# Transposing the softmax matrix by DMA instead of by matmul in a two-layer recurrent attention kernel

## The chip, the cores and the metric

The kernel runs on one core of a Trainium2 chip. The metric is device time in microseconds, the median of several runs; lower is better. A profiled execution gives the trace that is read here; its times are measured from the start of its span.

## What is computed

One block is a segment-recurrent attention followed by a gated feed-forward network (FFN), and it is applied twice with the same weights. The sequence has 2048 rows of 576 numbers, 32 heads of 128, an FFN of 4608.

```python
for s in range(n_seg):                     # 64 segments of 32 rows
    h = concatenate([mem, x[s]])           # 8 memory rows + 32 rows
    q, k, v = h @ Wq, h @ Wk, h @ Wv       # 32 heads of 128
    p = softmax(where(mask, q @ k.T * scale, -1e9))
    o = einsum(p @ v, Wo)
    mem = o[:8]                            # carried to the next segment
    outs.append(o[8:])
x = x + A(layernorm(x)); x = x + B(layernorm(x))    # B: (silu(x@w1) * (x@w3)) @ w2
x = x + A(layernorm(x)); x = x + B(layernorm(x))
```

Each segment needs the memory rows of the one before, so the attention is a chain of 64 links in each layer.

## The kernel before

**Steps.** The second layer runs eight segments behind the first (LAG). A step t does segment t of layer 0 and segment t - 8 of layer 1 together, 72 steps in all; in 56 of them both layers are there ("both"), in 16 one ("single"). The 32 heads are done in four groups of eight (g = 0 to 3). The FFN of finished rows, and the V of coming ones, are spread between the attention's pieces. The weights of the attention stay on the chip; those of the FFN are loaded again and again on SP's queue.

**A group.** Q and K are computed transposed into two PSUM banks (letters Q, and q for the contraction's tail), copied to QKT, and multiplied to scores (S). On VectorE and ScalarE follow the mask's addition, the row maximum and its subtraction, the exponential (sm_exp, on ScalarE), the row sum and its reciprocal, and the product with the reciprocal (sm_pb), which is written to PB, the softmax matrix P in bf16. In PB a row is a query (rows 0 to 39 are one layer's, 64 to 103 the other's) and a column is one of 128 rows of V, which hold both layers' keys and values in places that alternate with the step's parity (role). sm_pb writes only the columns of each row's own keys, in two to four instructions; the others must be zero.

**P transposed.** PV needs P with its keys on the partitions. ptr (letter T) does eight matmuls, PB as the stationary operand and fold, two 40 x 40 identities one above the other, as the moving one: the two layers' rows are added into the same 40 columns of one bank, 320 columns for eight heads. pt_ev evicts the bank twice, once for each layer, into PTS, each time times a column of slots (1 where the V row belongs to that layer, 0 elsewhere), on ScalarE or VectorE. In single steps it copies two halves of 160 columns with no mask. PV (P) then multiplies V by both layers' 80 columns; its result goes to OT, and Wo follows (O, tail o).

**Buffers.** PB has two buffers and PTS one. After each group's transpose GpSimd sets that PB to zero again (pb_zero, 128 x 1024).

**The order.** The program is a list of nodes with an engine, a duration, dependencies and buffers (make_nodes). plan (line 75) sends them out in time by an estimate; for TensorE the order is fixed by a string of letters (FIRST, then FOUR eleven times, then LAST), and every engine executes its nodes in the order that plan gives them. The letters are: m, a, b, n, p transposes of activations; Q q queries and keys; S scores; T the transpose of P; P P times V; O o the output projection; X x V v G g the values; F f the FFN's first matmuls; W w its second, for the two layers. FOUR covers four steps. Nodes marked AD go to ScalarE or VectorE, whichever plan finds free; the numbers in a node are plan's own estimates. A matmul node may use the whole array or column or row tiles of it; plan counts 0.098 us for a change (SWITCH).

All elementwise instructions are recorded at the two helper lines 594 (ScalarE) and 597 (VectorE), all matmuls at line 591. SP's DMAs are at line 600, those of ScalarE's queue at 603, which at present are four loads at the start, and those of GpSimd at 606.

Of the kernel before, what the change touches and what calls it, by code (L numbers as in the profile page):

```python
# [13 lines left out]
P = 128  # L14
# [20 lines left out]
POOLS = {"bank": 8, "qkt": 4, "sme": 2, "pb": 2, "pts": 1, "ot": 4,  # L35
# [158 lines left out]
def ewh(*ns):  # L194
# [5 lines left out]
    "maQQQqqQqqSQqTqSqQQQqSSvVXxPTPTOPOTOoPooOoQqqqqQQSQqqvSVQQTQSqqPQOTSPoXTOPToxPOOooQqqqqQQSQQSvqVQTqqQSQqPSaOTPTO"  # L200
    "PTooPOOooQQqqqqQSQVvSqqQQQqqQTSSPXTOPTOPoToxPOOooQQpQqqVvqqSnQQSfFFqqfQQqSTQqfPFTWPSFTOOooPFTffPOOooWQqqqqQQFSQF"
    "SQffqVvqqQWTQSFxfqfQFSPXTWPFTfOPOTFPOOooooWQqfqQQSFQfqqVvSQqqfFWTQqfQSFPQqfTOSPFOTWPFTOPfoooOoFfqqQQQSWQqqvVSFfq"
    "qQQTWqqSQQPTSOoPbaOTXPxTOPooxOoXqqpQQQSVqqnQvfFSTQqqQQPSFfqqfQTFOPSWTFfPOOTFPWOooooffFQQQqqqWSGFfgqQQqfFSTQPQQqq"
    "qfFSWGTSfgGPFggTGOPOTFPOOooooWVvfqqQQQSFqqffFQQWTSFfqqQPQfqqSFQWTOfPSTaFoOPWOTFPffFOoooWQQqqqqQSbQgqqGSQQTQPQTgq"
    "qSGSOPGggTGPOTOPoooOoQqqppQQQSvqqVnnQQqqSFSffqTFQPQqWTFSPffOwTFPOTFPOWOwooooFffqqQQQSWwQFfgqqGSFqqfQQTWQPQSFffqq"
    "FGTgSwPGfggTGPFTOPOWOOowoooFqqfQQwWQaQfqqSFSvVfqqQFQTFqqfPQTQwSWFSfPOOTFPwTWffFPOOooooWwqqqQQQbSQqqgqGSQTQPQQqgq"
    "TSGSGPggGTOPOTOPoooOo"
# [5 lines left out]
LAST = (  # L213
    "QQpQqqqQSqQpnQqqVvTSSnQFffqqFPQTOwPoSWTffFPFTOPOOoooFqqqfQQwWQQfqfSFSFqGQQqqgTQQPWwFqgfTSSGGPFfggfFTGOPOTWPOOwoF"
    "oooFfqqfQQQwvSqqVQQWQqqSFTSqfqQPQWTOPSwFTFPffOTOwPWOooooFFqqffQQwQQqqvSWVSFqqfQQTWPQTqqSVQvPOSTbOPxwOoTooPOoXqQp"
    "QpqqvVQSQqqnQnSQQqqFTSfqfPQTOPSFTFPOWTOPwOooooFqffqQQQSQQqqqvVSTQQqqFSffqFPQWSwTFPffTOPFOTwPOOoWoooFqfqqQQQFSQfq"
    "xvXVwWSTFPQffqqQWQTSwFFPfqqQOSwWTFOPffTFPOWOwooooFQQvfqqVqqQSQWFSwFffqqQQQSTWQqPqTPSOTOPowOToboPxOoXqqqQQQpSvVqq"
    "qQQSnQTFfqQFSPfqQOSTFfPowTFPfOTOPFOfooowQQqqqfQQSqFSVvqqQwQFTSQffqqQPFTSXPwTOPOTFPOOooooFfxfVvqqQQQSQqqqfQSFQqqq"
    "QSTQwSPFTOffPFTOPwTOPfooOooFQqqqQQSqqqQQSQvVQTSfFQqqPwTFSPfTOFPOTOPoofOoopwFnfffFFwFwfffFFFwffFFwffFFwffFFwfFffF"
    "wFwfffFFFfww"  # L220
# [11 lines left out]
def make_nodes(em, nseg, pools, o=Opt, dma_bw=230e3, load_bw=400e3):  # L232
# [26 lines left out]
    ld_m0 = node("ACT", 0.1, em.load_m0(), prio=-90, name="m0", lat=2.5)  # L259
    ld_t = [load("ldt", kb(3 * R64, 4096), -10.0, em.load_tails(0)), node("ACT", 0.1, em.load_tails(1), prio=-120, name="ldt", lat=6.0)]  # L260
    node("ACT", 0.1, em.load_tails(2), prio=-80, name="ldt", lat=6.0)
# [48 lines left out]
    def v_nodes(name, t, k, prio, tail_at, emit, strips, deps, tail_deps, free):  # L310

        modes = ("col", "quad") if strips[0][3] == R64 else ("c32", "oct")
        b = banks()
        m_ = node("PE", 8 * 0.2158, emit(b, False), deps=deps, prio=prio, mode=modes[0], acq=b, name=name)
        n = node("PE", 0.2158, emit(b, True), deps=deps + tail_deps, prio=prio + tail_at, mode=modes[1], acq=b, name=name + "t")
        reads_ht.setdefault(t, []).extend([m_, n])
        for r in (0, 1):
            outs = em.v_parts(strips, r)
            b[r].users = len(outs)
            for p0, width, row, blk in outs:  # L320
                e = node("AD", (0.49, 0.6), em.v_ev(b[r], p0, width, row, blk), deps=[m_, n] + free.get(blk // 2, []), prio=prio + 0.01 * (blk // 2),
                         rel=[b[r]], name=name + "e")
                vx_ev.setdefault((name, t, blk // 2), []).append(e)
        return [m_, n]
# [16 lines left out]
    def vg_out(t, g, b, deps, row):  # L341

        return [node("AD", (0.49, 0.6), em.v_ev(b[r], row, R64, row, 2 * g + r), deps=deps, prio=t + o.vm + 0.01 * g + (0.05 if row == 0 else 0.0), rel=[b[r]],
                     name="VGe") for r in (0, 1)]

    def vx_pair(t, prio):
# [5 lines left out]
        for k in ((0, 1) if both(t) else (0,)):  # L352
            v_nodes("VX", t, k, prio + 0.01 * k, o.vxt, (lambda k: lambda b, tail: em.vx(t, k, b, tail))(k), em.vx_strips(t, k), deps, [], free)

    def step(t):
# [17 lines left out]
        for g in range(NG):  # L373
# [52 lines left out]
            me[f"SC{g}"], me[f"TR{g}"], me[f"PV{g}"], me[f"WO{g}"] = sc, tr, pv, wo  # L426
# [100 lines left out]
    def x_in(g):  # L527
        xn = Slot("xn")
        ld = node("DMA" if g else "ACT", 0.8 if g else 0.1, em.load_xn(g, xn), deps=reads_ht.get(4 * g - 3, [])[:1], prio=4 * g - 3.0 if g else -100, acq=[xn],
                  name="ldxn", lat=2.5)  # L530
# [31 lines left out]
SW = 2 * QW  # L562

# [4 lines left out]
class Emitter:  # L568
# [431 lines left out]
    def sm_pb(self, t, g, sme, pb):  # L1000
        def f(n):
            for kd, key, c0, w in self.p_at(t):
                rs = slice(64 * kd, 64 * kd + QW)
                X, rec = self.T.SME[rs, sme.i], self.T.STAT[rs, sme.i]
                self.v("tensor_tensor", self.T.PB[rs, pb.i, :, c0:c0 + w], X[:, :, key:key + w],
                       rec.unsqueeze(2).to_broadcast([QW, GH, w]), op=ALU.mult)
        return f

    def pb_zero(self, pb):
        return lambda n: self.ch("POOL", self.nc.gpsimd.memset(self.T.PB[:, pb.i], 0.0))  # L1010
# [4 lines left out]
    def ptr(self, t, g, pb, b):  # L1015

        def f(n):
            for j in range(GH):
                self.mm(self.bk(b)[:, j * QW:(j + 1) * QW], self.T.PB[0:104, pb.i, j, :], self.T.fold[0:104, :], True, True)
        return f  # L1020

    def pt_ev(self, t, g, m, b, pts):

        def f(n):
            src = self.bk(b)[:, 0:GH * QW]
            if not self.both(t):
                w = 4 * QW
                self.cp(n, self.T.PTS[:, pts.i, 0, m * w:(m + 1) * w], src[:, m * w:(m + 1) * w])
                return
            dst = self.T.PTS[:, pts.i, m, :]  # L1030
            keep = self.T.slots[:, role(t), m ^ role(t):(m ^ role(t)) + 1]
            if n.by == "ACT":
                self.act(dst, src, ACT.Copy, scale=keep)
            else:
                self.v("tensor_scalar", dst, src, keep, None, op0=ALU.mult)
        return f
# [75 lines left out]
    def yts(self, t, ls, tail):  # L1112
        def f(n):
            yT, _ = self.yT(t)
            for li in ls:
                j = (t - LAG * li) % 4
                c0 = self.ycol(t, self.kind(t, li), False)
                if not tail:
                    self.cp(n, self.T.YTS[:, li, 0:4, j * SEG:(j + 1) * SEG], yT[:, 0:4, c0:c0 + SEG])
                else:  # L1120
                    self.v("tensor_tensor", self.T.YTS[R64:P, li, 4, j * SEG:(j + 1) * SEG], yT[0:R64, 4, c0:c0 + SEG],
# [3 lines left out]
    def post_tr(self, li, g, b):  # L1125
        def f(n):

            for db in (4, 3, 2, 1, 0):
                d0 = min(db * P, D - P)
                self.mm(self.bk_bf(b, D)[:, d0:d0 + P], self.T.YTS[:, li, db, :], self.T.ident[:, 0:P], True, True, is_transpose=True)  # L1130
# [79 lines left out]
def kernel(  # L1210
# [41 lines left out]
    T.fold = sp.tile([P, QW], BF, name="fold")  # L1252

    T.slots = sp.tile([P, 2, 2], F32, name="slots")

# [16 lines left out]
    T.YO = sp.tile([R64, 2 * QW], F32, name="YO")  # L1272
    T.YTS = sp.tile([P, 2, 5, P], BF, name="YTS")
# [11 lines left out]
    nc.gpsimd.memset(T.fold[:], 0.0)  # L1285
    for r in (0, R64):
        nc.gpsimd.affine_select(out=T.fold[:], in_=T.fold[:], compare_op=ALU.not_equal, fill=1.0, base=-r,
                                pattern=[[-1, QW]], channel_multiplier=1)

    nc.gpsimd.memset(T.slots[:], 0.0)  # L1290
    for e, kd, lo, hi in ((0, 1, 24, 80), (1, 0, 72, 112)):
        inside, outside = T.slots[:, e, kd:kd + 1], T.slots[:, e, 1 - kd:2 - kd]
        nc.gpsimd.memset(inside, 1.0)
        nc.gpsimd.affine_select(out=inside, in_=inside, compare_op=ALU.is_ge, fill=0.0, base=-lo, pattern=[[0, 1]], channel_multiplier=1)
        nc.gpsimd.affine_select(out=inside, in_=inside, compare_op=ALU.is_ge, fill=0.0, base=hi - 1, pattern=[[0, 1]], channel_multiplier=-1)
        nc.gpsimd.tensor_scalar(outside, inside, -1.0, 1.0, op0=ALU.mult, op1=ALU.add)

# [54 lines left out]
```

## Time and profile before

| | before |
|---|---|
| runs, median (lowest to highest) | 2704.19 us (2703.2 to 2704.23) |
| profiled execution | 2708.0 us |
| its span | 2705.0 us |
| mean granted TensorE clock | 0.997 |
| HBM read | 308.49 MB, 115 GB/s over the span |
| share of the 16 DMA engines taken by SP's queue | 38.5% |
| stretch 0 to 250 us: PE busy | 211.1 us |
| stretch 250 to 2415 us (both layers): PE busy | 2135.6 of 2165.0 us |
| stretch 2415 to 2705 us: PE busy | 271.9 us |

The span runs from the first to the last instruction of the program. PE is TensorE's matmuls, PEld its weight loads, which overlap them, DVE VectorE, ACT ScalarE, POOL GpSimd, SP the queue that issues most DMAs; a q behind a name is that engine's sequencer. A group of instructions is named by what it writes, an arrow, and what it reads; after the bar stand its busy time and the mean length of one, then the idle time of the engine just before them and what ended it. The chain of work is followed back from the last instruction to whatever released each. Matmuls are pipelined, so a busy TensorE is not yet one at its peak.

### The profile page before, as it was taken

The numbers are of one execution on the slowest core, as the hardware profiler recorded it, in microseconds if no ns is written. First come the engines' busy times: TensorE is split into PE (matmuls) and PEld (weight loads), VectorE is DVE, ScalarE is ACT, GpSimd is POOL, SyncE is SP. The second block draws the span as 40 slices with busy tenths as digits, with TensorE's granted clock in tenths as the row PEclk, the third lists the DMA queues.
The fourth block names the chain that finished last, engine by engine and source line by source line (L and its number), as shares of the span: only waits on it lengthen the run. The fifth ranks groups of instructions, "written<-read, shape, count | busy, mean of one in ns | idle before, by whom it ended". The sixth has DMA issues, their size and how long they took to land.

```text
span 2705.0 us, 135792 instructions
## 1 busy us (share of the span) xinstructions
PE 2618.6 (97%) x60482; PEld 2272.3 (84%) x60523; DVE 2097.7 (78%) x5423; ACT 1401.6 (52%) x3978; POOL 334.1 (12%) x411
## 2 busy tenths in 40 slices
PE   5999999999999999999999999999999999999998
PEld 4788888888888888888888888888888888888886
DVE  5777887787788778777877877787777777777876
ACT  2655554554555555554555555455545546554452
POOL 1111110110111011011101101010111101011110
PEclk9999999999999999999999999999999999999999
DMA  9064524244342434434243433423343342334457
GB/s 316 7 182 118 158 82 128 80 119 116 104 124 85 116 90 119 117 108 128 76 119 88 127 108 108 134 80 110 94 124 106 108 139 70 112 93 130 129 166 245
DMA packets 478171, 321.99 MB, mean 119 GB/s; under 512 B 26024, under 2 KB 467760, under 8 KB 476944
## 3 DMA queue, kind: packets, MB, share of 16 engines
q1 hardware_dynamic: 474048, 305.43, 38.5%
q8 instruction: 473, 7.75, 1.2%
q0 software_dynamic: 3024, 6.93, 0.9%
q10 hardware_dynamic: 512, 0.94, 0.2%
q14 instruction: 114, 0.93, 0.1%
HBM read 308.49 MB, written 2.36 MB: 115 GB/s over the span
## 4 chain that ended last, share of the span: by engine, by line
PE 80%; DVE 9%; ACT 6%; issue 2%; DMA 2%; SPq 1%; POOL 0%; ACTq 0%; DVEq 0%; POOLq 0%
PE bank L591 80%; ACT V L594 3%; DVE STAT L597 2%; DVE PTS L597 2%; ACT PTS L594 1%; DVE V L597 1%; DVE SME L597 1%; DVE PB L597 1%; DMA W<-in_A_Wk_dram 1%; DVE HTT L597 1%; SPq L600 1%; DMA W<-in_B_w_dram 1%; ACT HT L594 0%; ACT QKT L594 0%; DMA WV<-in_A_Wv_dram 0%
## 5 line engine op out<-in xcount | busy, mean ns | idle before, releaser
L591 PEld LDWEIGHTS <-W 128*128 128x128 bf16 (+2 forms) x31904 | 1258.2, 100 | 128.8 <-issue 68.7
L591 PE MATMUL bank<-HT,W 128*128 128x80 bf16 (+3 forms) x23040 | 799.9, 196 | 16.8 <-issue 7.3
L591 PE MATMUL bank<-XTB,W 128*64 128x256 bf16 (+5 forms) x8864 | 662.6, 263 | 5.9 <-DMA W<-in_B_w_dram 3.0
L594 ACT ACTIVATE QKT<-bank 128x256 bf16<-128x256 f32 (+2 forms) x1524 | 349.5, 311 | 363.5 <-PE bank L591 320.7
L1010 POOL MEMSET PB<- 128x1024 bf16 x288 | 273.9, 951 | 1944.5 <-PE bank L591 1242.7
L591 PE MATMUL bank<-OT,WO 128*128 128x80 bf16 (+2 forms) x11520 | 401.6, 198 | 2.2 <-issue 1.8
L594 ACT ACTIVATE V<-bank 32x512 bf16<-32x512 f32 (+1 forms) x609 | 347.8, 586 | 90.4 <-PE bank L591 81.6
L591 PEld LDWEIGHTS <-WO 128*128 128x128 bf16 (+1 forms) x11520 | 376.8, 102 | 13.7 <-issue 4.4
L591 PE MATMUL bank<-WV,HT 128*32 128x512 bf16 (+5 forms) x3728 | 362.3, 381 | 3.8 <-issue 2.2
L591 PE MATMUL bank<-W2C,HTT 128*128 128x288 bf16 (+1 forms) x2776 | 318.4, 286 | 2.9 <-issue 1.8
L597 DVE TENSOR_REDUCE STAT<-SME 104x8 f32<-104x320 f32 (+1 forms) x576 | 274.0, 476 | 25.2 <-ACT SME L594 18.9
L597 DVE TENSOR_TENSOR PB<-SME,STAT 40x128 bf16<-40x128 f32 (+4 forms) x912 | 275.5, 336 | 9.7
L594 ACT ACTIVATE HTT<-bank 128x512 bf16<-128x512 f32 (+1 forms) x324 | 175.3, 550 | 185.9 <-PE bank L591 183.9
L591 PEld LDWEIGHTS <-HT 128*32 128x32 bf16 (+4 forms) x3768 | 164.1, 99 | 119.5 <-issue 20.3
L597 DVE SCALAR_TENSOR_TENSOR XR<-bank,XR 128x288 f32<-128x288 f32 x576 | 243.7, 448 | 23.3 <-PE bank L591 17.4
L591 PEld LDWEIGHTS <-HTT 128*128 128x128 bf16 (+1 forms) x2840 | 222.4, 103 | 42.2 <-issue 4.5
L597 DVE SCALAR_TENSOR_TENSOR HTT<-HTT,bank 128x512 bf16<-128x512 bf16 (+1 forms) x324 | 201.0, 620 | 59.0 <-ACT HTT L594 56.2
L594 ACT ACTIVATE OT<-bank 128x320 bf16<-128x320 f32 (+1 forms) x392 | 147.0, 403 | 173.0 <-PE bank L591 146.3
L597 DVE CAST QKT<-bank 128x192 bf16<-128x192 f32 (+4 forms) x524 | 140.5, 315 | 117.7 <-PE bank L591 117.3
L597 DVE TENSOR_TENSOR HTT<-HTT,bank 128x512 bf16<-128x512 bf16 (+1 forms) x324 | 203.6, 628 | 28.5 <-PE bank L591 0.9
L594 ACT ACTIVATE PTS<-bank,slots 128x320 bf16<-128x320 f32 x315 | 157.0, 531 | 128.8 <-PE bank L591 95.0
L594 ACT ACTIVATE SME<-SME 104x320 f32<-104x320 f32 (+1 forms) x288 | 135.5, 470 | 100.2 <-DVE SME L597 95.5
(69 smaller groups left out, 1856.8 us busy)
## 6 DMA issues: line engine op xcount, KB each, us to landing
W<-in_B_w_dram SPq DMA_DIRECT2D x612, 256.0 KB, 3.6
W2C<-in_B_w_dram SPq DMA_DIRECT2D x306, 288.0 KB, 3.3
W<-in_B_w_dram SPq DMA_DIRECT2D x612, 32.0 KB, 3.5
W<-in_B_w_dram SPq DMA_DIRECT2D x8, 1024.0 KB, 12.2
W<-in_A_Wq_dram SPq DMA_DIRECT2D x9, 512.0 KB, 9.5
WO<-in_A_Wo_dram SPq DMA_DIRECT2D x4, 1152.0 KB, 16.7
XR<-in_A_x_dram POOLq DMA_DIRECT2D x16, 288.0 KB, 2.8
WV<-in_B_w_dram SPq DMA_DIRECT2D x4, 1152.0 KB, 10.9
```

The lines of the kernel that those rows point to most:

```text
L591: self.ch("PE", self.nc.tensor.matmul(out, lhsT=lhsT, rhs=rhs, start=start, stop=stop, skip_group_check=True, **k))
L594: self.ch("ACT", self.nc.scalar.activation(*a, **k))
L597: self.ch("DVE", getattr(self.nc.vector, fn_)(*a, **k))
L600: self.ch("SP", self.nc.sync.dma_start(out=out, in_=in_))
L1010: return lambda n: self.ch("POOL", self.nc.gpsimd.memset(self.T.PB[:, pb.i], 0.0))
```

## The change

- In steps with both layers P is no longer transposed by matmuls. One DMA for each group, issued from ScalarE's queue, transposes PB's first 112 rows (PQ) into PTS: for each of the eight heads 112 columns, of which 0 to 39 are one layer's queries and 64 to 103 the other's. The two layers stay apart, so fold, slots, the masked evictions and the letters T of these steps go. PV reads the two column blocks of each head by an access pattern, in the order that the step's parity asks for (pcols).
- In single steps T stays, with the identity as moving operand, and one eviction copies all 320 columns, where two copied 160 each.
- PB has one buffer, PTS two. PB is set to zero once a step, before group 0's sm_pb, after the last transpose of the step before, since within a step all groups write the same columns.
- YO, a small scratch tile, now lies within YTS, whose layout is changed for it.
- The TensorE order is new throughout, and some of plan's estimates are others (those of the loads at the start, of V's evictions, of the new DMA: 0.45 us on ScalarE and 2.6 us until it has landed).

```diff
+TRD, TRL = 0.45, 2.6
-POOLS = {"bank": 8, "qkt": 4, "sme": 2, "pb": 2, "pts": 1, "ot": 4,
+POOLS = {"bank": 8, "qkt": 4, "sme": 2, "pb": 1, "pts": 2, "ot": 4,
...
 FOUR = (
-    "QqqpQQpQqqVvnSSnQFfqfqFQQQTfqqSFPWTFPSwTfFOOPWTwPOOooooFqqffQQQQfqqSFGSgqfFTQQPwQTQqqqgGSWPFGSfggfFOTGPOwTOPWOoo"
-    "ooFqfqqQQwWQQVqvSaSFFffqqQQwQQqqSTWSFPffTFOPWwTOFPffTOFPwWOooooFfqqqQQWQQSqqqQSQQbQqgqSTGGPSgTGPOTggGPOTwPOOoooo"
+    "QQppQqqqqQvVSnnSQFffqqFQQSFfqqPQFWSwPFfPOOwOPWOooooFqffqQQQQqqfSFWGSFfgqqQQPQQqqgSGSwPGFfggfFOGPOWPOOoowooFvqqQQ"
+    "QQqfqVwSSWFFqfqfQQQQqqSPWwFSffPFOWOPFwOffPFOoaoowWoFfqqqQQWSQQqqqQSQbQQgqqSGwSPgGgGgPGOPOPOOoooo"
 )
...
             pb = Slot("pb")
+            if g == 0 and t:
+                zero = [node("POOL", 0.95, em.pb_zero(pb), deps=last_pt, prio=pf, acq=[pb], name="pbz")]
+            else:
+                zero = []
...
-            pbs = node("DVE", w, em.sm_pb(t, g, sme, pb), deps=[d], prio=pf, acq=[pb], rel=[sme], name="pb", lat=0.125 if nl == 2 else 0.225)
+            pbs = node("DVE", w, em.sm_pb(t, g, sme, pb), deps=[d] + zero, prio=pf, acq=[pb], rel=[sme], name="pb", lat=0.125 if nl == 2 else 0.225)
             pts = Slot("pts")
-            bt = Slot("bank", users=2)
-            tr = node("PE", 8 * 0.0258, em.ptr(t, g, pb, bt), deps=[pbs], prio=pf + o.tr, mode="full/col", acq=[pts, bt], name="TR")
-            node("POOL", 0.95, em.pb_zero(pb), deps=[tr], prio=pf, rel=[pb], name="pbz")
-            pe_ = [node("AD", (0.425, 0.46) if nl == 2 else ew(160), em.pt_ev(t, g, m, bt, pts), deps=[tr], prio=pf, rel=[bt], name="PTe") for m in (0, 1)]
+            if nl == 2:
+                pe_ = [node("ACT", TRD, em.ptd(t, g, pb, pts), deps=[pbs], prio=pf, acq=[pts], rel=[pb], name="TRD", lat=TRL)]
+                last_pt[:] = pe_
+            else:
+                bt = Slot("bank")
+                tr = node("PE", 8 * 0.0258, em.ptr(t, g, pb, bt), deps=[pbs], prio=pf + o.tr, mode="full/col", acq=[pts, bt], rel=[pb], name="TR")
+                pe_ = [node("AD", ew(320), em.pt_ev(t, g, bt, pts), deps=[tr], prio=pf, rel=[bt], name="PTe")]
+                last_pt[:] = [tr]
...
+    def ptd(self, t, g, pb, pts):
+        return lambda n: self.ch("ACT", self.nc.scalar.dma_start(out=self.T.PTS[:, pts.i], in_=self.pbt(pb)[0:PQ].rearrange("p h k -> p (h k)"),
+                                                                 transpose=True))
...
-                        self.T.PTS[:, pts.i, 0:nq // QW, j * QW:(j + 1) * QW], True, True)
+                        self.pcols(t, pts, j), True, True)
...
+    def pcols(self, t, pts, j):
+        P_ = self.T.PTS[:, pts.i, j, :]
+        if not self.both(t):
+            return P_[:, 0:QW]
+        v, e = P_[:, 0:1], role(t)
+        return bass.AP(v.tensor, v.offset + R64 * e, [list(x) for x in v.ap][:-1] + [[R64 - P * e, 2], [1, QW]])
...
-    T.PB = sp.tile([P, pools["pb"], GH, P], BF, name="PB")
-    T.PTS = sp.tile([P, pools["pts"], 2, GH * QW], BF, name="PTS")
+    T.PB = sp.tile([P, GH, P], BF, name="PB")
+    T.PTS = sp.tile([P, pools["pts"], GH, PQ], BF, name="PTS")
```

More of the change, by code (lines that the diff above doesn't have):

```diff
@@ L215 @@
[L215 to L219, printed above, removed]
@@ L221 @@
+    "TQPFSfOwTfFPOTOPFOoooowQfqqfFQQSQvqqVqqQQSwTSQqfqQFTSfXPFPTOFwTOPxooPOOooFfVqfvqQQQSQqqqFSQQfqqqQTSwQfTPSFFPOOfT"
+    "woToPFfPOOooQQqqqQQSqQSqqvQVQSqfTFqQFTSPPwTOOfPTPOoooOofpwfFFnfFFwfffFFwFwfffFFFwfffFFwFwfffFFFwffFFwfffFFww"
 )
@@ L257, in load @@
         return node("DMA", nbytes / load_bw, fn, deps=deps, prio=prio, name=name, lat=2.0)
-    ld_m0 = node("ACT", 0.1, em.load_m0(), prio=-90, name="m0", lat=2.5)
-    ld_t = [load("ldt", kb(3 * R64, 4096), -10.0, em.load_tails(0)), node("ACT", 0.1, em.load_tails(1), prio=-120, name="ldt", lat=6.0)]
-    node("ACT", 0.1, em.load_tails(2), prio=-80, name="ldt", lat=6.0)
+    node("DMA", 4.0, lambda n: None, prio=-999.0, name="boot")
+    ld_m0 = node("ACT", 0.6, em.load_m0(), prio=-90, name="m0", lat=8.0)
+    ld_t = [load("ldt", 1.7 * kb(3 * R64, 4096), -10.0, em.load_tails(0)), node("ACT", 0.6, em.load_tails(1), prio=-120, name="ldt", lat=8.0)]
+    node("ACT", 0.6, em.load_tails(2), prio=-80, name="ldt", lat=10.0)
     ld_h = [load("ldqk", kb(512, 4096), half - 9.0, em.load_qk(half)) for half in (0, 1)]
@@ L320, in v_nodes @@
             for p0, width, row, blk in outs:
-                e = node("AD", (0.49, 0.6), em.v_ev(b[r], p0, width, row, blk), deps=[m_, n] + free.get(blk // 2, []), prio=prio + 0.01 * (blk // 2),
+                e = node("AD", (0.56, 0.6), em.v_ev(b[r], p0, width, row, blk), deps=[m_, n] + free.get(blk // 2, []), prio=prio + 0.01 * (blk // 2),
                          rel=[b[r]], name=name + "e")
@@ L341, in vg_out @@
     def vg_out(t, g, b, deps, row):
-        return [node("AD", (0.49, 0.6), em.v_ev(b[r], row, R64, row, 2 * g + r), deps=deps, prio=t + o.vm + 0.01 * g + (0.05 if row == 0 else 0.0), rel=[b[r]],
+        return [node("AD", (0.56, 0.6), em.v_ev(b[r], row, R64, row, 2 * g + r), deps=deps, prio=t + o.vm + 0.01 * g + (0.05 if row == 0 else 0.0), rel=[b[r]],
                      name="VGe") for r in (0, 1)]
@@ L528, in x_in @@
         xn = Slot("xn")
-        ld = node("DMA" if g else "ACT", 0.8 if g else 0.1, em.load_xn(g, xn), deps=reads_ht.get(4 * g - 3, [])[:1], prio=4 * g - 3.0 if g else -100, acq=[xn],
-                  name="ldxn", lat=2.5)
+        ld = node("DMA" if g else "ACT", 0.8 if g else 0.6, em.load_xn(g, xn), deps=reads_ht.get(4 * g - 3, [])[:1], prio=4 * g - 3.0 if g else -100, acq=[xn],
+                  name="ldxn", lat=2.5 if g else 9.0)
         ht_set(0, g, ln_nodes("L0", xn, xn, [ld], 4 * g - 2.0 if g else -8, ht_writes(0, g)))
@@ L562 @@
 SW = 2 * QW
+PQ = 112
 X_AT = (24, 104)
@@ L1004, in f, with pbt @@
                 X, rec = self.T.SME[rs, sme.i], self.T.STAT[rs, sme.i]
-                self.v("tensor_tensor", self.T.PB[rs, pb.i, :, c0:c0 + w], X[:, :, key:key + w],
+                self.v("tensor_tensor", self.pbt(pb)[rs, :, c0:c0 + w], X[:, :, key:key + w],
                        rec.unsqueeze(2).to_broadcast([QW, GH, w]), op=ALU.mult)
         return f
+    def pbt(self, pb):
+        return self.T.PB[:]
     def pb_zero(self, pb):
-        return lambda n: self.ch("POOL", self.nc.gpsimd.memset(self.T.PB[:, pb.i], 0.0))
+        return lambda n: self.ch("POOL", self.nc.gpsimd.memset(self.pbt(pb), 0.0))
+    def ptd(self, t, g, pb, pts):
+        return lambda n: self.ch("ACT", self.nc.scalar.dma_start(out=self.T.PTS[:, pts.i], in_=self.pbt(pb)[0:PQ].rearrange("p h k -> p (h k)"),
+                                                                 transpose=True))
     def nq(self, t):
@@ L1018, in f, with pt_ev @@
             for j in range(GH):
-                self.mm(self.bk(b)[:, j * QW:(j + 1) * QW], self.T.PB[0:104, pb.i, j, :], self.T.fold[0:104, :], True, True)
+                self.mm(self.bk(b)[:, j * QW:(j + 1) * QW], self.pbt(pb)[0:104, j, :], self.T.ident[0:104, 0:QW], True, True)
         return f
[L1022 to L1036, printed above, removed]
+    def pt_ev(self, t, g, b, pts):
+        return lambda n: self.cp(n, self.T.PTS[:, pts.i, :, 0:QW], self.bk(b)[:, 0:GH * QW].rearrange("p (h q) -> p h q", h=GH))
     def pv(self, t, g, pts, b):
@@ L1129, in f @@
                 d0 = min(db * P, D - P)
-                self.mm(self.bk_bf(b, D)[:, d0:d0 + P], self.T.YTS[:, li, db, :], self.T.ident[:, 0:P], True, True, is_transpose=True)
+                self.mm(self.bk_bf(b, D)[:, d0:d0 + P], self.T.YTS[:, 4 * li + db if db < 4 else 8 + li, :], self.T.ident[:, 0:P], True, True, is_transpose=True)
         return f
@@ L1250 @@
     T.ident = sp.tile([P, P], BF, name="ident")
-    T.fold = sp.tile([P, QW], BF, name="fold")
-    T.slots = sp.tile([P, 2, 2], F32, name="slots")
     T.maskb = sp.tile([P, 2, QW], BF, name="maskb")
@@ L1284 @@
                             pattern=[[-1, P]], channel_multiplier=1)
[L1285 to L1296, printed above, removed]
     nc.gpsimd.memset(T.maskb[:], 0.0)
```

32 lines of the change are left out of this document (17 added, 15 removed).

## Prediction

> **What bounds the kernel now.** I read the head of the page, then the summary of the chain that ended last, to see which engine sets the end.
>
> ```profile
> PE 2618.6 (97%) x60482; PEld 2272.3 (84%) x60523; DVE 2097.7 (78%) x5423; ACT 1401.6 (52%) x3978; POOL 334.1 (12%) x411
> ...
> PE 80%; DVE 9%; ACT 6%; issue 2%; DMA 2%; SPq 1%; POOL 0%; ACTq 0%; DVEq 0%; POOLq 0%
> ```
>
> TensorE is busy 97% of the span and makes 80% of the chain; the rest is mostly short pieces of VectorE and ScalarE for which TensorE has little else to do. Next the table by stretches, for one round of four steps in the middle (the order string FOUR, played 11 times; the rounds from 1483.87, 1640.93 and 1797.99 us each take 157.06 us).
>
> ```profile
> 1483.87:1640.93 157.06, 155.22 (x3449) 136.16 (x3449) 124.16 (x319) 83.45 (x234) 18.55 (x22) 1.00 0.38 108
> ```
>
> The columns are length, busy PE, PEld, DVE, ACT, POOL, granted clock, DMA share, GB/s. TensorE is idle 1.84 us of 157.06, at full clock. So only less work on TensorE, or fewer stretches in which it runs below its pace, shortens a round. Then the timeline of one group's P, the fourth of a step.
>
> ```profile
> 1506.06 1.13 DVE L597 TENSOR_TENSOR PB<-SME,STAT 40x128 bf16<-40x128 f32 x4
> ...
> 1507.38 0.37 PEld L591 LDWEIGHTS <-PB 104*128 104x128 bf16 x8
> 1507.50 0.36 PE L591 MATMUL bank<-fold,PB 104*128 104x40 bf16 x8
> 1507.68 0.85 PEld L591 LDWEIGHTS <-HTT 128*128 128x128 bf16 x8
> 1507.70 1.14 PE L591 MATMUL bank<-W2C,HTT 128*128 128x288 bf16 x8
> ...
> 1507.89 0.53 ACT L594 ACTIVATE PTS<-bank,slots 128x320 bf16<-128x320 f32 x1 [0.91 <-PE bank L591]
> ...
> 1508.45 0.55 DVE L597 TENSOR_SCALAR PTS<-bank,slots 128x320 bf16<-128x320 f32 x1 [0.26 <-ACT PTS L594]
> ...
> 1509.06 0.45 PE L591 MATMUL bank<-PTS,V 128*128 128x80 bf16 x8 [0.21 <-DVE PTS L597]
> ```
>
> PB is complete at 1507.19 and PV starts at 1509.06, 1.87 us later. The eight transposing matmuls hold TensorE from 1507.50 to 1507.70 (the next node's first matmul), 0.20 us. PV then waits 0.21 us for the second eviction: this path has no slack here.
>
> **TensorE work removed.** The letters T fall from 288 to 64, so 224 groups lose their matmuls. Over the 223 groups between 250 and 2415 us, first transposing matmul to first matmul of the next node is 0.21 us at the median where there are 8 matmuls, 0.25 where there are 16, and 55.9 us in all. The floor is some 47 us (224 x 0.21); I take 52. Node lengths read in the same way (medians, us: Q 1.15, q 0.15, S 0.24, P 0.28, O 1.15, o 0.14, F 1.76, f 0.23, W and w 0.98, G 1.72, g 0.23, V 1.84, v 0.34, T 0.21) sum over the old FOUR to 148.9, over the new one to 145.5; the round took 157.06. The 8.2 us between are waits and changes between row, column and full tiles: by the letters 55 changes a round before, 59 after. Four more cost from nothing to 4 x 0.15 (8.2/55); I take 0.1 each, over 56/4 = 14 rounds **+6** (0 to +8).
>
> **Evictions, masks, zeros.**
>
> ```profile
> L1010 POOL MEMSET PB<- 128x1024 bf16 x288 | 273.9, 951 | 1944.5 <-PE bank L591 1242.7 <-DVE SME L597 242.3 <-DVE HTT L597 140.9
> ...
> L594 ACT ACTIVATE PTS<-bank,slots 128x320 bf16<-128x320 f32 x315 | 157.0, 531 | 128.8 <-PE bank L591 95.0 <-DVE PTS L597 23.7 <-ACT V L594 7.1
> ...
> L597 DVE TENSOR_SCALAR PTS<-bank,slots 128x320 bf16<-128x320 f32 x133 | 73.2, 550 | 41.0 <-ACT PTS L594 38.9 <-PE bank L591 0.6
> ```
>
> These groups of instructions (shapes kept apart; busy us and mean ns after the bar) lose 157.0 us on ACT and 73.2 on DVE, per group 0.70 and 0.33. ACT gets 224 DMA issues instead: the four that it issues before the first matmul take 0.58 to 0.83 us each, the 1,592 on SP 0.47 at the median, so 105 to 130 us of queue. ACT and DVE both come out lighter; ACT's idle 48% and DVE's 22% hide the issues, so **0** in itself. If that cover failed, half a microsecond a group, 112 us, would reach the path. POOL loses 217 of 288 memsets of 0.951 us; POOL is idle 88%, so 0. The one zeroing left in a step waits for the last landing of the step before and needs 0.95 us, while the next group's PB is written ten and more microseconds later (at 1490.77 us, after a last PV at 1471.48, in the round shown): hidden. The constants fold and slots leave POOL's first 7.4 us, before the first matmul at 10.51 that waits for a DMA: 0, within 2 us either way, with the swapped first two letters.
>
> **The new wait.** PV now waits for the DMA. Before, 224 groups with both layers had 4.74 us on average (4.76 median) from the end of PB to the first PV matmul; a tenth had under 2.31, the least 1.54. No transposing DMA is in the trace; the nearest rows are these.
>
> ```profile
> W<-in_B_w_dram SPq DMA_DIRECT2D x612, 256.0 KB, 3.6
> W2C<-in_B_w_dram SPq DMA_DIRECT2D x306, 288.0 KB, 3.3
> ...
> XR<-in_A_x_dram POOLq DMA_DIRECT2D x16, 288.0 KB, 2.8
> ...
> XN<-in_A_x_dram SPq DMA_DIRECT2D x15, 144.0 KB, 3.7
> ```
>
> The last column is issue to landing. P is 112 x 1024 x 2 bytes, 224 KB, on ACT's own queue beside the weight bursts: XR, on a queue of its own, bounds it below at 2.7 (its fastest), the slowest tenth of the 256 KB loads above at 4.9. I take 3.3, and with 0.3 for semaphores on both sides (the 0.21 above and some for ACT's turn) the path from PB to PV needs 3.6 us; ends 2.8 and 5.2. Had every PV stayed where it is, the sum over groups of what is missing would be 25 us at 2.8, 69 at 3.6, 140 at 4.6. But the new order gives more room: by the same node lengths, scores to PV is 9.2 us against 8.5 at the shortest tenth, 10.2 against 9.8 at the quarter, and DVE is freed of 0.33 us a group, some 1.0 us together. So I read the table 1.0 lower: 17 us at 2.6. **+20** (0 to +100).
>
> What queues behind: ACT's issue waits for DVE's PB and a free PTS buffer, and exps, QKT and OT evictions stand behind it; TensorE waits for those. DVE's next PB waits for the landing, since there is one PB, with the next group's maxima behind it; PB writes followed each other within 4 us in 70 of 223 cases before. ACT and DVE have 83.45 and 124.16 of 157.06 us to do, so a shift passes unless it lands on an exp that is due.
>
> **Single steps**: 64 groups evict once (320 columns, like OT's 0.44 to 0.49 us) instead of two halves side by side of 0.30: 0.15 to 0.2 later. All on the path would be 13; with TensorE's waits there I take **+3**.
>
> **Sum**: -52 + 6 + 0 + 20 + 3 = -23 us. The profiled execution took 2708.0 (span 2705.0 and 3.0 around it), which gives 2685; the runs' median is 2704.19, so **2681**.
>
> **Rivals.** *It lands late (slower, 0.25).* The place is the PV of a step's last group: in the new FOUR's first step, scores to PV is 8.2 us by the letters, while the fastest chain from scores to PB's end took 4.6 and the median one 7.0. For: weights arrive in bursts, the digits of the round's 40 slices being
>
> ```profile
> DMA  0544384634550174126241533977555000001430
> ```
>
> so half of the transposes meet slices at 4 tenths or more. Against: the mean share is 0.38. With 4.6 to land and 0.3, the need is 4.9; read at 3.9 the table says 89, sum +46 to 2750. It decides from a wait of 41 us, a need of some 4.2 us from PB's end. *ACT is held while it issues (slower, 0.15).* If pushing out a transpose takes ACT's queue not 0.5 but some 2 us, the landing moves 1.5 later: need 5.1, read at 4.1, 103 us, and exps behind it slip too; +60 to 2764, up to 2850. Against: no issue on ACT exceeds 0.83 us in this trace; for: none of them transposes. [...] *Nothing is left (same, 0.07)*: the wait eats what T gave; 2704. It needs the wait to fall within 41 us by some 5 either way.
>
> **How the numbers follow.** The forecast has 0.53; its own range is 2642 (-56 for T, no wait, no changes, single steps free) to 2698. No change means within 0.2%, 2698.8 to 2709.6, about what runs of this kernel can tell. Faster 0.53, same 0.07, slower 0.40. The late landing reaches to 2790 (need 5.2 and some held issues), so 2640 to 2790 leaves out about a tenth above and little below.
>
> **What would show it.** Right: a round near 154 us; no PB matmul in both-layer steps; PE's waits for PTS small; issue to landing near 3.3; ACT's issue near 0.5. Wrong: PE idle before PTS,V matmuls by a DMA of over 40 us in all; DVE idle before PB writes; ACT's issue instruction of over a microsecond, or exps waiting on ACT while their input has long been there. If issue to landing exceeds 4 us, the forecast is wrong.

## The result, and the profile after

The changed kernel takes 2789.32 us at the median (2783.99 to 2789.97, four runs), the one before 2704.21 (2703.20 to 2704.58, four runs): a ratio of 1.0311, 95% interval 1.0293 to 1.0329, so 85 us slower. The profiled execution took 2789.97 us, its span 2788.2.

First the head of the page of the changed kernel, the queue that the transposing DMAs are on (packets, MB, share of the 16 DMA engines), and the chain that ended last.

```profile
PE 2611.6 (94%) x58881; PEld 2252.3 (81%) x58913; DVE 2048.6 (73%) x5228; ACT 1234.8 (44%) x3661; POOL 130.5 (5%) x182
...
q10 hardware_dynamic: 208384, 52.35, 12.3%
...
PE 54%; DVE 17%; DMA 14%; issue 7%; ACT 5%; ACTq 2%; SPq 1%; POOL 0%; DVEq 0%; POOLq 0%
PE bank L602 54%; DMA PTS<-PB 12%; DVE PB L608 4%; DVE STAT L608 3%; DVE SME L608 3%; DVE HTT L608 2%; DVE V L608 2%; ACTq L1027 2%; ACT V L605 1%; DVE QKT L608 1%; ACT QKT L605 1%; DVE XR L608 1%; SPq L611 1%; ACT HTT L605 1%; DMA W<-in_A_Wk_dram 1%
```

Every engine has less to do than before, and the span is longer. TensorE's share of the chain fell from 80 to 54%; the transposing DMA, which was not there, is 12% of it, and VectorE grew from 9 to 17%. Next one round of four steps in the table by stretches (length, busy PE, PEld, DVE, ACT, POOL, granted clock, DMA share, GB/s).

```profile
1861.44:2023.79 162.35, 153.32 (x3343) 133.73 (x3341) 120.38 (x305) 71.62 (x216) 7.50 (x10) 1.00 0.53 127
```

The round took 157.06; here it takes 162.35, and the rounds, which were equal, now run from 159.0 to 167.2. TensorE is idle 9.0 us instead of 1.84, at full clock in this one, and the DMA share rose from 0.38 to 0.53. The groups of instructions that write PB and read PTS (busy us, mean ns, then idle time just before them and what ended it), and the view of the tile PTS (issue instruction: ns least/median/longest; issue to landing in us):

```profile
L608 DVE TENSOR_TENSOR PB<-SME,STAT 40x128 bf16<-40x128 f32 (+4 forms) x912 | 275.0, 335 | 66.0 <-DMA PTS<-PB 58.9
...
L602 PE MATMUL bank<-PTS,V 128*128 128x80 bf16 (+3 forms) x2848 | 133.3, 199 | 84.8 <-DMA PTS<-PB 62.5
```

```profile
L1027 ACTq DMA_TRANSPOSE PTS<-PB x224: 1237/1240/2629, 247.2 to 2498.1; - x112
...
DMA to landing us min/median/max: 2.6/3.9/8.1
```

Two engines wait for the same landing: TensorE 62.5 us before PV, and VectorE 58.9 us before it may write the next PB. One place shows it whole; this is the timeline (start, length, engine, line, operation; in brackets the idle time before it and its releaser).

```profile
904.93 1.24 ACTq L1027 DMA_TRANSPOSE PTS<-PB  x1
...
905.73 4.97 SPq L611 DMA_DIRECT2D W<-in_B_w_dram  x4
...
908.14 0.60 ACT L605 ACTIVATE HTT<-bank 128x512 bf16<-128x512 f32 x1 [0.56 <-PE bank L602]
908.23 0.20 DVE L608 RECIPROCAL STAT<-STAT 104x8 f32<-104x8 f32 x1
912.63 0.53 PEld L602 LDWEIGHTS <-V 128*128 128x128 bf16 x8 [4.81 <-DMA PTS<-PB]
912.64 0.71 PE L602 MATMUL bank<-PTS,V 128*128 128x80 bf16 x8 [4.53 <-DMA PTS<-PB]
912.68 1.12 DVE L608 TENSOR_TENSOR PB<-SME,STAT 40x128 bf16<-40x128 f32 x4 [4.25 <-DMA PTS<-PB]
...
913.12 0.77 ACT L605 ACTIVATE OT<-bank 128x320 bf16<-128x320 f32 x2 [4.38 <-PE bank L602]
...
913.84 1.24 ACTq L1027 DMA_TRANSPOSE PTS<-PB  x1
```

The transpose is issued at 904.93; from 905.73 four weight loads follow on SP's queue; it lands near 912.6, 7.7 us after its issue. Then PV and the next sm_pb start together. VectorE had the next group's reciprocal ready at 908.43 and could not write PB, since there is one; so that group's own transpose is issued only at 913.84. The same place in the table by stretches:

```profile
906.00:908.00 2.00, 2.00 (x36) 1.62 (x32) 1.97 (x6) 1.24 (x3) 0.00 (x0) 1.00 0.97 204
910.00:912.00 2.00, 0.00 (x0) 0.00 (x0) 0.00 (x0) 0.00 (x0) 0.00 (x0) 0.93 0.55 133
913.00:914.00 1.00, 1.00 (x19) 1.00 (x17) 0.96 (x4) 0.77 (x2) 0.00 (x0) 0.50 0.07 21
917.00:918.00 1.00, 1.00 (x13) 0.81 (x11) 0.00 (x0) 0.00 (x0) 0.66 (x1) 0.50 0.00 0
920.00:924.00 4.00, 4.00 (x104) 3.74 (x102) 1.47 (x4) 0.90 (x3) 0.00 (x0) 1.00 0.37 104
```

The granted clock falls to half shortly before 912, some 3.6 us after TensorE's last matmul, and stays there for 6.8 us, in 5.9 of which TensorE works. Over the whole trace the matmuls bank<-OT,WO of 128x80 start every 67 ns at the median at half clock and every 36 at full, so the stand of 4.5 us costs, by estimate, about 3 more in slow matmuls. In the steps with both layers the trace has seven such stretches, 37.5 us long together, by the same estimate up to 18.8 us of the loss; before there was none. All seven begin at marks that lie 3.41 us or a multiple of it apart, and in the 3.41 us ahead of each TensorE stood 1.9 to 3.4 us; ahead of the marks where the clock stayed full it stood 1.8 us at most.

All of the loss lies in the steps with both layers: from the first scores of step 8 to those of step 64 the kernel before needs 2182.1 us, the changed one 2267.7, 85.6 more. Cut into nodes (a node's first matmul to the next one's first, so that a wait is counted with the node ahead of it) the difference is T -56.3; O +33.3, Q +32.1, f +31.3, F +19.3, S +19.1, P +9.6, g +6.9, W and w +1.8, q -5.4, all others -6.

### The profile page after: what moved, and what is told of

It is laid out like the page before. It is cut to its first block, busy times and chain, and to the rows that moved or that the text cites. A ratio compares the mean times of both kernels' runs of the same rounds, so it can differ in the third digit from the quotient of the medians.

```text
span 2788.2 us, 132271 instructions
## 1 busy us (share of the span) xinstructions
PE 2611.6 (94%) x58881; PEld 2252.3 (81%) x58913; DVE 2048.6 (73%) x5228; ACT 1234.8 (44%) x3661; POOL 130.5 (5%) x182
## 4 chain that ended last, share of the span: by engine, by line
PE 54%; DVE 17%; DMA 14%; issue 7%; ACT 5%; ACTq 2%; SPq 1%; POOL 0%; DVEq 0%; POOLq 0%
PE bank L602 54%; DMA PTS<-PB 12%; DVE PB L608 4%; DVE STAT L608 3%; DVE SME L608 3%; DVE HTT L608 2%; DVE V L608 2%; ACTq L1027 2%; ACT V L605 1%; DVE QKT L608 1%; ACT QKT L605 1%; DVE XR L608 1%; SPq L611 1%; ACT HTT L605 1%; DMA W<-in_A_Wk_dram 1%
## 5 line engine op out<-in xcount | busy, mean ns | idle before, releaser
L602 PE MATMUL bank<-OT,WO 128*128 128x80 bf16 (+3 forms) x11520 | 419.6, 200 | 5.5 <-ACT OT L605 3.9
L602 PEld LDWEIGHTS <-WO 128*128 128x128 bf16 (+1 forms) x11520 | 396.1, 103 | 23.9 <-issue 10.8
L605 ACT ACTIVATE V<-bank 64x512 bf16<-64x512 f32 (+1 forms) x563 | 322.3, 587 | 165.2 <-PE bank L602 99.2
L602 PE MATMUL bank<-WV,HT 128*32 128x512 bf16 (+3 forms) x3642 | 370.9, 385 | 3.4 <-issue 2.4
L602 PE MATMUL bank<-W2C,HTT 128*64 128x288 bf16 (+1 forms) x3424 | 323.2, 287 | 2.4 <-DVE HTT L608 1.5
L608 DVE TENSOR_TENSOR PB<-SME,STAT 40x128 bf16<-40x128 f32 (+4 forms) x912 | 275.0, 335 | 66.0 <-DMA PTS<-PB 58.9
L602 PEld LDWEIGHTS <-HTT 128*64 128x64 bf16 (+1 forms) x3488 | 239.6, 107 | 37.3 <-issue 6.7
L608 DVE CAST V<-bank 64x512 bf16<-64x512 f32 (+1 forms) x301 | 206.3, 686 | 21.2 <-PE bank L602 15.5
L602 PE MATMUL bank<-PTS,V 128*128 128x80 bf16 (+3 forms) x2848 | 133.3, 199 | 84.8 <-DMA PTS<-PB 62.5
L608 DVE CAST QKT<-bank 128x192 bf16<-128x192 f32 (+2 forms) x457 | 124.4, 317 | 116.3 <-PE bank L602 114.8
L602 PEld LDWEIGHTS <-V 128*128 128x128 bf16 (+1 forms) x2848 | 107.0, 104 | 116.0 <-DMA PTS<-PB 46.9
## 6 DMA issues: line engine op xcount, KB each, us to landing
W<-in_B_w_dram SPq DMA_DIRECT2D x8, 1024.0 KB, 12.1
```

Of the source, the lines that this page charges most:

```text
L602: self.ch("PE", self.nc.tensor.matmul(out, lhsT=lhsT, rhs=rhs, start=start, stop=stop, skip_group_check=True, **k))
L605: self.ch("ACT", self.nc.scalar.activation(*a, **k))
L608: self.ch("DVE", getattr(self.nc.vector, fn_)(*a, **k))
```

## The experiments

The expectations set several theories against one another: that the new order and the fewer buffers cost the time (O); that PV's wait for the landing does (L1); that VectorE's wait for the one PB does; that ScalarE's queue does, held by the issue or standing until PB is there; and, across these, that the weights' traffic makes the landing late. Each kernel was run beside the one before on the same chip, whose medians lay between 2703.66 and 2704.71 us.

**The order alone, with no DMA (e1).**

```diff
     def ptd(self, t, g, pb, pts):
-        return lambda n: self.ch("ACT", self.nc.scalar.dma_start(out=self.T.PTS[:, pts.i], ..., transpose=True))
+        return lambda n: None
...
+    nc.vector.memset(T.PTS[:], 0.01)
```

> The transposing DMA is left out: in steps with both layers PV multiplies V by a PTS that is filled once at the start, so P of these steps is missing from the output. Every engine has the same order as the changed kernel. Late landing (theory L: PV and the next PB wait for a DMA that lands at 3.9 us median instead of 3.05) and held queue (theory H: 1.24 us of ScalarE's queue per issue instead of 0.45) both say that order and buffers alone keep the saving: 2640 to 2665 us. New order (theory O: the letters themselves, 59 tile changes a round, are the loss) says 2750 us or more.

Measured: 2626.34 us, 0.9714 of before (0.9700 to 0.9729), 14 us under the lowest that was expected. Its page, engines and chain:

```profile
PE 2568.2 (98%) x58881; PEld 2229.7 (85%) x58913; DVE 2042.4 (78%) x5229; ACT 1245.3 (47%) x3661; POOL 130.4 (5%) x182
...
PE 87%; DVE 7%; DMA 2%; ACT 2%; issue 1%; SPq 1%; ACTq 0%; DVEq 0%
```

Theory O falls. With P transposed for nothing, the new order would be 77 us faster, and TensorE sets the end more than before. The DMA has cost 163 us.

**The DMA runs, nobody reads it or waits with PB for it (e2).** It reads a part of WO that never changes and writes PTS; PV reads WO.

```diff
-        ... in_=self.pbt(pb)[0:PQ].rearrange("p h k -> p (h k)"), transpose=True))
+        ... in_=self.T.WO[0:PQ].rearrange("p h d -> p (h d)")[:, 0:GH * P], transpose=True))
...
-        v, e = P_[:, 0:1], role(t)
+        v, e = self.T.WO[:, j, 0:1], role(t)
```

> The DMA is issued at the same places and of the same size, but from a constant (WO) into PTS, which PV of both-layer steps does not read (it reads WO), so P of these steps is missing from the output; nobody waits for a landing. What is left is ScalarE's held queue and the DMA traffic. H: nearly all of the loss is still there, 2740 to 2790 us. L: 2650 to 2685 us, within 25 us of the kernel without the DMA. Issue instruction about 1.24 us, landing like that of the changed kernel (2.6 alone, 4 to 8 beside weights).

Measured: 2638.85 us, 0.9757 (0.9736 to 0.9777). The issues and their traffic by themselves cost 12.5 us, though each issue holds ScalarE's queue for 1.24 us at the median and lands after 4.3.

**PV doesn't wait, PB does (e5).** The DMA is the real one; only PV reads WO, the second half of the edit of e2.

> The DMA transposes the real PB into PTS as in the changed kernel, but PV of both-layer steps reads a constant (WO), so P of these steps is missing from the output. Only PV's wait for the landing is gone; ScalarE still stands before each issue until PB is written, and VectorE's next PB still waits for the landing. If PV's wait on TensorE is the loss (L1): 2640 to 2670 us, near the run with the unread DMA (2639). If the waits in ScalarE's and VectorE's queues are (L2): 2720 to 2780.

Measured: 2741.28 us, 1.0133 (1.0114 to 1.0151). L1 falls as the whole cause: PV's wait is worth 48.0 us (2789.32 less 2741.28), and the kernel is still slower than before. In its view of waits (us in total, times, longest):

```profile
DVE PB L608 <- DMA PTS<-PB: 55.1, 45, 3.9
```

VectorE's wait is as it was, 55.1 us against 58.9. ScalarE stands too: ahead of its issues it is idle for 186.5 us in all, and each issue follows PB's end by 0.03 to 0.08 us. What this kernel has beyond e2 is these two waits, ScalarE's for PB and VectorE's for the landing. Together they cost 102.4 us (2741.28 less 2638.85).

**ScalarE waits for a part of PB, PB is free at once (e9).** As e2, with one element of PB copied on ScalarE just ahead of the issue. This was meant to make ScalarE wait for sm_pb as in the changed kernel, and does so in part only. The element is in row 0, column 0: in half of the steps the second of sm_pb's four instructions writes it, in the other half none of its three does.

```diff
+            self.act(self.T.mem0T[0:1, 0, 0:1], self.pbt(pb)[0:1, GH - 1, 0:1], ACT.Copy)
             self.ch("ACT", self.nc.scalar.dma_start(out=self.T.PTS[:, pts.i], in_=self.T.WO[0:PQ]...
```

> As the run in which PV does not wait (2741 us), but the DMA's source is a constant (WO) and ScalarE reads one element of PB just before the issue, so it still stands until PB is written, while VectorE's next PB has no landing to wait for; P of both-layer steps is missing from the output, and 0.2 us of ScalarE a group comes on top. If ScalarE standing before PB (A) is the loss: 2715 to 2750 us. If VectorE's wait for the one PB (D) is: 2640 to 2670 us.

Measured: 2648.48 us, 0.9797 (0.9781 to 0.9814). That is 9.6 us over e2, the copies themselves among it; the view of waits shows how long ScalarE stands before them:

```profile
ACT mem0T L605 <- DVE PB L608: 61.1, 49, 2.6
```

All of this but 0.1 us lies in the one half of the steps, and there the copy starts 0.5 us before PB is complete (median); in the other half 53 of 112 copies start before sm_pb's first instruction has ended. Over all groups the issue comes 0.95 us before PB's end on average, against 1.53 before in e2 and 0.04 after in e5. So e9 holds about a third of ScalarE's standing, and 9.6 us is not its price. What e5 has beyond this kernel, 92.8 us (2741.28 less 2648.48), is VectorE's wait for the landing and the rest of ScalarE's standing. The two were not told apart, and they feed each other: ScalarE stands for a PB that VectorE may not write yet. So the DMA's price, taken apart in this order:

| what is added | time | step |
|---|---|---|
| no DMA (e1) | 2626.3 | |
| the DMA's issues and traffic (e2) | 2638.9 | +12.5 |
| ScalarE waits for a part of PB (e9) | 2648.5 | +9.6 |
| ScalarE waits for all of PB, VectorE's next PB for the landing (e5) | 2741.3 | +92.8 |
| PV waits for the landing (changed kernel) | 2789.3 | +48.0 |

The last two hold clock as well: half-clock stretches with both layers amount to none in e9, 20.5 us in e5 and 37.5 in the changed kernel, of which up to half is lost: by estimate some 10 us and some 9 us of the two steps. The parts were added in this one order; another could divide them otherwise.

**No weight loads (e4), and the same on the kernel before (c1).** The FFN's weights W13 and W2C stay at a constant.

```diff
-        def f(n): ...
+        return lambda n: None
...
+    nc.vector.memset(T.W13[:], 0.01)
+    nc.vector.memset(T.W2C[:], 0.01)
```

> The FFN's weight loads of all rounds but the last are left out (the two weight tiles are filled once at the start), so the FFN is not the reference's. The transposing DMA has the DMA engines to itself. If the weights' traffic makes the landing late (L by contention): landings all near 2.63 us and 2660 to 2710 us. If the hold (H) or the order (O) costs the time: 2750 us or more with the same landings.

> A control: the kernel before without the FFN's weight loads of all rounds but the last (tiles filled once), so its FFN is not the reference's. If the loads cost only where a transposing DMA shares the engines with them: 2690 to 2706 us, no change. If the run without loads was faster for other reasons: below 2650.

Measured: e4 2693.03 us, 0.9958 (0.9943 to 0.9973); c1 2694.89, 0.9962 (0.9947 to 0.9977). From the view of PTS of e4, and its waits:

```profile
DMA to landing us min/median/max: 2.6/2.6/5.0
```

```profile
PE bank L602 <- DMA PTS<-PB: 16.5, 16, 2.2
...
DVE PB L608 <- DMA PTS<-PB: 5.7, 9, 1.4
```

Without the loads the kernel before gains 9.8 us, the changed one 96.3. So some 86 us of the loss comes from transposes that meet weights: without the loads they land after 2.6 us at the median (a tenth still after more than 4.1), and VectorE's wait falls from 58.9 to 5.7. Still the two are level without loads: on ScalarE's queue the transposes then earn 2 us, no more than the measurement tells from nothing, though TensorE and VectorE wait for landings by only 22 us in all. ScalarE stands for 170.7 us before its issues here.

**The DMA on SP's queue (e11), and that without weight loads (e12).** In the plan it becomes a node of a queue of its own; it is issued by SyncE, behind the loads issued earlier. The orders of ScalarE and VectorE change a little with it; 18 instructions go from the one to the other.

```diff
-                pe_ = [node("ACT", TRD, em.ptd(t, g, pb, pts), ...
+                pe_ = [node("TRQ", TRD, em.ptd(t, g, pb, pts), ...
...
-        return lambda n: self.ch("ACT", self.nc.scalar.dma_start(...
+        return lambda n: self.ch("SP", self.nc.sync.dma_start(...
```

> The changed kernel with the transposing DMA issued from SP's queue, among the weight loads in the order of the plan's times; result as the reference's. ScalarE neither holds nor stands. If A is the larger part of the queues' 102 us: 2690 to 2735 us. If D is: 2760 to 2790. If SP's own in-order waits for weight buffers delay the issue: above 2790, with PB's end to the issue no longer 0.04 us.

> The transposing DMA issued from SP's queue, and the FFN's weight loads of all rounds but the last left out (so its FFN is not the reference's): no hold on ScalarE and no traffic beside it, landing 2.6 us at the median. Beside the same without loads from ScalarE's queue (2693): if holding and standing on ScalarE cost by themselves, 2640 to 2665 us; if what SP's queue gained (84 us) was only a faster landing beside the weights, 2685 to 2700.

Measured: e11 2705.53 us, 1.0004 (0.9988 to 1.0020), 84 us less than on ScalarE's queue and within the range for ScalarE's standing as the larger part; e12 2661.54, 0.9840 (0.9826 to 0.9854), within the range for holding and standing that cost by themselves. The view of PTS and the waits of e11:

```profile
L1027 SPq DMA_TRANSPOSE PTS<-PB x224: 1222/1240/2317, 246.4 to 2415.3; - x112
...
DMA to landing us min/median/max: 2.6/2.9/5.8
```

```profile
PE bank L602 <- DMA PTS<-PB: 45.8, 56, 2.3
...
DVE PB L608 <- DMA PTS<-PB: 21.8, 26, 1.5
```

PB to issue grows from 0.04 to 0.28 us on average, and yet the landing comes sooner: 2.9 us from issue at the median instead of 3.9 (3.3 and 3.9 on average; the traces show 139 and 197 landings of 224), the longest 5.8 instead of 8.1. Without loads, where both land after 2.6 at the median, SP's queue is 31.5 us faster (2693.03 less 2661.54), although TensorE and VectorE wait longer for landings there, 23.0 and 12.1 us against 16.5 and 5.7. That is what ScalarE's queue gives back when it need neither stand nor push, the changed orders included. It is more than the 22 us of the table (12.5 and 9.6), another sign that e9 holds too little of the standing. The rest of the 84, some 52 us, was not taken apart: the landing comes earlier, and beside the loads ScalarE's standing may cost more as well. Why a transpose lands sooner behind the loads of one queue than beside them from another was not taken further.

**The order before, with the DMA (e8).** The letters of the kernel before, less the T of steps with both layers; all else as in the changed kernel.

> The changed kernel with the letters of the kernel before, from which only the T of both-layer steps are taken out. There PB's end to PV was 4.7 us on average, a tenth under 2.3, where the landing takes 3.9. If the new letters' extra room for the wait is worth much: 2820 to 2900 us. If the letters don't matter: 2780 to 2800. If they cost (O): below 2770.

Measured: 2908.82 us, 1.0743 (1.0700 to 1.0787). PV's wait in its view of waits:

```profile
PE bank L637 <- DMA PTS<-PB: 152.2, 86, 4.9
```

With the DMA the new letters are worth 119.5 us, and PV's wait, 152.2 us against 62.5, says that much of it is their room for the landing. This kernel has 92.2 us of half-clock stretches with both layers, against 37.5.

**The plan is told the measured times (e3).** `TRD, TRL = 1.24, 2.65` for 0.45 and 2.6; the letters stay.

> Only the plan's two numbers for the DMA change, 0.45 and 2.6 us to 1.24 and 2.65 (the measured issue and the rest of the median landing of 3.9); TensorE's letters stay, ScalarE's and VectorE's orders follow. If the loss comes from ScalarE and VectorE standing in the wrong order behind a wait that plan did not see (L or H through in-order queues), 2700 to 2760 us. If it is the landing on the path itself or TensorE's letters, no change: 2780 to 2795 us.

Measured: 2852.71 us, 1.0552 (1.0533 to 1.0570), 63 us worse than the changed kernel: a miss. With the letters fixed the estimate only moves work between and within ScalarE and VectorE. PV's wait rose:

```profile
PE bank L602 <- DMA PTS<-PB: 90.2, 59, 4.3
```

from 62.5, and the half-clock stretches from 37.5 to 81.9 us. Which moved instruction begins it stays open.

**One eviction in single steps (e7).** On the kernel before: 320 columns once, where it copies 160 twice.

```diff
-                w = 4 * QW
-                self.cp(n, self.T.PTS[:, pts.i, 0, m * w:(m + 1) * w], src[:, m * w:(m + 1) * w])
+                self.cp(n, self.T.PTS[:, pts.i, 0, :], src)
```

> One part of the change alone, on the kernel before: single steps evict P by one instruction of 320 columns in place of two halves. 64 groups, 0 to 0.2 us later each: 2703 to 2716 us.

Measured: 2705.31 us, 1.0003 (0.9994 to 1.0012). It is worth nothing either way.

**Matmul for a step's last group, DMA from SP's queue for the other three (e13).** To the changed kernel's letters one T a step is added, put some 1.5 us of TensorE's work ahead of its PV, with fold and the masked evictions of the kernel before.

```diff
-            if nl == 2:
+            if nl == 2 and g in (0, 1, 2):
...
-                pe_ = [node("AD", ew(320), em.pt_ev(t, g, bt, pts), ...
+                pe_ = [node("AD", (0.425, 0.46) if nl == 2 else ew(320), em.pt_ev(t, g, m, bt, pts), ...) for m in range(nl)]
```

> Result as the reference's: the DMA from SP's queue for groups 0 to 2 of a step, the matmuls with masked evictions of the kernel before for group 3, whose letter T is put 1.5 us of TensorE's work ahead of its PV. 56 groups pay 0.25 us of TensorE again, +14 us; the shortest waits from PB to PV are gone. If PV's wait in group 3 is the larger part of what is left in the SP version (2705): 2680 to 2700 us, faster than both kernels. If not: 2705 to 2725.

Measured: 2692.06 us (2683.99 to 2698.05, six runs), 0.9953 (0.9936 to 0.9970): 12 us faster than the kernel before, 97 faster than the changed one, and it leaves out nothing of the computation. The chain of its page, its landings, and its waits:

```profile
PE 75%; DVE 11%; DMA 8%; issue 3%; ACT 2%; SPq 1%; POOL 0%; ACTq 0%; DVEq 0%; POOLq 0%
```

```profile
DMA to landing us min/median/max: 2.9/3.0/4.9
```

```profile
DVE PB L643 <- DMA PTS<-PB: 28.0, 29, 2.3
...
PE bank L637 <- DMA PTS<-PB: 16.0, 16, 2.3
```

TensorE is at 75% of the chain again. The transposes still have 8% of it. PV's wait fell from e11's 45.8 us to 16.0; VectorE's, 28.0, is no shorter than e11's 21.8, and the kernel is ahead all the same.

## Why the prediction was wrong, step by step

- **What bounds the kernel: right.** Without the DMA (e1) less TensorE work is less time, one for one and more: PE is busy for 50.4 us less (2618.6 less 2568.2), and the kernel is 77.5 us faster.
- **TensorE work removed, -52: right.** The nodes T shrank by 56.3 us, the upper figure of the working. e1's gain of 77.5 is 21 more, although the sum counted 6 the other way for changes of tile. PV's waits for the evictions, which e1 has not, and the second buffer of PTS may make this up; they were not told apart.
- **Evictions, masks and zeros, 0: right in sum, the size of the issue wrong.** ScalarE lost 166.8 us of busy time, VectorE 49.1, GpSimd 203.6. The issue takes 1.24 us at the median, not the 0.47 to 0.83 of plain DMAs, and 310 us of queue in all; where nobody waits, issues and traffic cost 12.5 us (e2).
- **The new wait, +20: the right place, mis-sized.** It measured +48.0 (changed kernel less e5). The landing was taken at 3.3 us and has a median of 3.89; a tenth take over 5.46. The bounds from the nearest rows, 2.7 and 4.9, held the middle but not the tail, and the tail is what waits. The table was read 1.0 lower for the new order's room; the new letters' worth is real and larger than that (119.5 us, e8). The half-clock stretches, too, were 17 us longer with PV's wait than without (37.5 against 20.5 in e5), and no term of the sum had that.
- **What queues behind: this step failed.** It named both waits ("ACT's issue waits for DVE's PB" and "DVE's next PB waits for the landing, since there is one PB"), gave them no term in the sum and let a shift pass "unless it lands on an exp that is due", because ACT and DVE have 83.45 and 124.16 of 157.06 us to do. The share of busy time was the wrong measure: both engines take their instructions in the plan's order, so behind the standing sm_pb stand the next group's maxima, the FFN's products and the residuals XR, and behind ScalarE's issue its evictions, TensorE's own inputs among them. The two waits cost 102.4 us (e5 less e2), twice PV's. How much of that is VectorE's and how much ScalarE's stays open: e9 has about a third of ScalarE's standing for 9.6 us, while without loads taking the transposes off ScalarE's queue was worth 31.5 (e4, e12).
- **Single steps, +3: 0** (e7, within 0.12%).
- **The sum.** -23 was expected, +85 came. The measured parts are -77.5 for the matmuls, evictions and order (e1), +12.5 for issues and traffic (e2), +102.4 for the two waits in the queues (e5) and +48.0 for PV's wait, together +85.
- **It lands late:** it does land late, and 2750 was nearer than the forecast, but its place was PV of a step's last group alone, and PV's wait is worth 48 over all groups. **ACT is held:** the hold is there, but no run shows the some 2 us that its sum takes for every issue: here it takes 1.24 us at the median, 2 us or more in 16 of 224, and where nobody waits for the landing it costs 12.5 us with its traffic, not 60. **Nothing is left** fits the DMA on SP's queue, not this kernel. The rival that was missing is a mechanism by itself: one PB, handed back only when the landing is in, with VectorE and then ScalarE standing for it in turn.
- **The signs named beforehand** were right: TensorE waits for PTS by 62.5 us where 40 was the limit, VectorE idles ahead of PB, the issue is over a microsecond. The median landing of 3.89 stayed just under the 4 us that were to make the forecast wrong; a median says too little here. The range held the time by 0.7 us, which is luck: its upper end was made from PV's late landing and some held issues, not from what happened.

A second PB beside the two PTS, which would part VectorE's wait from ScalarE's, was not tried.

## What to carry to other kernels

Where a DMA takes over work that an engine did in place, ask first how long it keeps its source and who stands at its issue: here, with a single buffer, the engine that writes the source waited 58.9 us for the landing, the engine that issues stood for 186.5 us until the source was written (e5), and what was behind them in both queues waited with them, though VectorE was busy for 73% of the span and ScalarE for 44%. Price a landing by its slow tenth beside the kernel's own traffic (here over 5.46 us where the median was 3.89), and a stand of TensorE by more than its length where the granted clock falls after it (here after 1.9 us or more of the 3.41 ahead of a mark). Before giving up such a change, try its issue from another queue and keep the old way for the one place where the result is needed soonest; here that turned 85 us lost into 12 won.

## What the hardware showed that was not expected

- One transpose of 112 x 1024 bf16 is 896 packets of 256 bytes and 32 small ones. It landed no sooner than 2.6 us after its issue, within 2.75 in two thirds of the cases without weight loads (e4), and up to 8.1 us beside them. Where the loads took less than 0.5 us of the 16 DMA engines' time in its first 2.63 us, the mean was 3.3 (105 transposes of the changed kernel), where over 2 us, 5.9 (nine).
- Its issue takes 1.24 us of the queue at the median, on ScalarE's and, in e11, on SP's, and up to 2.6 (2.9 in e9). In 209 of the 224 issues of the changed kernel ScalarE began no other instruction meanwhile.
- In the steps with both layers the granted clock fell to 0.50 at marks 3.41 us or a multiple of it apart, where TensorE stood 1.9 to 3.4 us of the 3.41 ahead (seven times in the changed kernel) or 2.0 to 3.2 (six times in e5). Where TensorE stood less than that, up to 1.8 us in the one and 1.96 in the other, the clock stayed full. The fall lasted for 3.4 us (three of the seven stretches) or 6.8 (four).
